# A Fourier transform woven into a gated MLP: the next batch's folds and second-stage calls are put at other steps

## The chip, the cores and the metric

The kernel runs on one core of one Trainium2 chip. The metric is the device time of one execution in microseconds (us), the median over the runs shown. The engines are named as in the profile: PE is TensorE (PEld its weight loads), DVE is VectorE, ACT is ScalarE, POOL is GpSimd, SP is SyncE, which here only issues DMAs. L285 means line 285 of the kernel before.

## The reference, cut to what matters

```python
def _attn_ref(x):                       # x: 8 x 3008 x 256, float32
    X = np.fft.fft(x, axis=1)
    X = np.fft.fft(X, axis=2)
    return X.real.astype(np.float32)

def _moe_ref(x, w_in, w_out):           # x: 24064 x 256, w_in: 256 x 2048, w_out: 2048 x 256
    h = x @ w_in
    g = h * np.cos(h)
    return (g @ w_out).astype(np.float32)
```

The second function is applied to the result of the first, reshaped to 24064 rows of 256.

## The kernel before, in words

**Tiling.** The 8 batches are worked on one after the other. The Fourier transform along the sequence (3008 = 64 x 47) is done in two stages by matmuls with constant matrices; the transform along the 256 columns is folded into `w_in`. Symmetries leave 6 groups of columns per batch (`NG = 6`): group 0 is 225 wide, groups 1 to 5 are 256 wide (`_width`). Each group is passed through the MLP in 8 steps, each with 256 of the 2048 hidden units. So a batch has 48 steps, the kernel 384; below, "index" is the number of a step within its batch, 0 to 47, and group g holds the indices 8g to 8g+7.

**One step.** The main loop (line 741) writes out by hand the order of the instructions of step t; each engine takes its own instructions in that order, and instructions of different engines are tied by waits on the data alone. In step t:

- `mm1(cur, 0)`: two PE matmuls with `WC` into the PSUM tile `H`, which ACT has seeded (L453). `act_e` (L494): ACT copies 2H into `ew`. Then, after four matmuls of another step, `mm1(cur, 1)`: two matmuls with `WS` into the same `H`; they wait until ACT's L494 has read `H`.
- `dve_h` (L499): DVE computes `h = ew - H`. `act_round` (L514): ACT rounds `H` and then `h`, the second half of the work in `h` and both after `dve_h`.
- For the step before: `dve_frac` (L518, twice, one operand `H` in PSUM or `h` in SBUF) and `act_sin` (L524). For the step before that: `dve_g` (L528, twice, again with `H` or `h`) and `dve_s` (L539, L546, L548), differences of SBUF tiles.
- For step t-3: `mm2`, seven PE matmuls into four PSUM banks that accumulate over the 8 steps of a group (L572).

**At the end of a group** (the step whose t-3 or t-4 was a group's last, that is, index 2 and 3 modulo 8): `take_m` (L593) copies the sums from PSUM by ACT, and `combine_m` (L611 to L621) forms the output sums `cb` by six additions on POOL, called at index 3 modulo 8. `store_out`, called at index 4 and at index 5 modulo 8, transposes `cb` on DVE (L664) and issues the output DMAs on SP (L674).

**The next batch's transform.** While batch b is in the MLP, batch b+1 is transformed. `transform(b)` (L360) lists calls with the index of the step at whose end they are put:

- `load_x` (L159): two halves of x, by DMA on SP.
- 8 chunks c, each of 4 of the 32 positions: `fold(b, c, e)` (L240), for e = 0 and 1 one POOL addition or subtraction of 110 x 508 from `xp` into the single buffer `xf`, and with e = 0 an ACT copy of column 0 (L247). `first_half` (L285): PE matmuls from `xf` into the PSUM tile `pz`; ACT copies it to `zs` (L290, L291). For c = 0 and 4 it also runs `middle` (L255, L263). A fold of the next chunk must wait until PE has read `xf`.
- `store_z` (L307): four DMAs on SP per chunk, to DRAM. `load_z` (L316): two DMAs back, as the tile `z2`.
- `second_half(b, g)` (L327): four PE matmuls (eight records) into `pb`, one ACT copy to `pq` (two for g = 0), and two DMAs on SP (L349, L350) that spread one row of it over 128 partitions as `nb`. `pq` and `nb` are what group g of the next batch starts from: `seed` needs `nb` in the step before the group's first.

`pz` and `pb` share one PSUM bank. Batch 0's own transform is done ahead of the loop, but for five `second_half` calls at its indices 5, 10, 14, 18 and 22 (`opening`). Batch 7 has no next batch.

Of the kernel before, what the change touches and what calls it, by code (L numbers as in the profile page):

```python
# [29 lines left out]
NG = 6  # L30
# [91 lines left out]
def kernel(  # L122
# [8 lines left out]
    NB = x.shape[0]  # L131
# [221 lines left out]
    def spread_norm():  # L353
        T = _width(0)
        pq, nb = ready[0, 0]
        pn = psum("pn", "M")
        nc.tensor.matmul(pn[:, 0:T], lhsT=ones, rhs=pq[0:1, T : 2 * T], start=True, stop=True)
        nc.scalar.copy(out=nb[:, 0:T], in_=pn[:, 0:T])

    def transform(b):  # L360
        todo = {}

        def at(o, *call):
            todo.setdefault(o, []).append(call)

        at(3, load_x, b, 0)
        at(14, load_x, b, 1)
        for q in range(4):
            for c, o, f in ((2 * q, 6, 8), (2 * q + 1, 9, 13)):
                at(8 * q + o, fold, b, c, 0)  # L370
                at(8 * q + o, fold, b, c, 1)
                at(8 * q + f, first_half, b, c)
                at(8 * q + f + 1, store_z, b, c, 0)
                at(8 * q + f + 1, store_z, b, c, 1)
        at(39, load_z, b, 0)
        at(39, load_z, b, 1)
        for g in range(NG):
            at(42 + g, second_half, b, g)
        return todo

    def fold_weights(e, n, tag="M"):
        W = WS if e else WC
        pw = psum("pw", tag)
        for i in range(2):
            nc.tensor.matmul(
                pw,
                lhsT=CS[i][:, 128 * e : 128 * e + 128],
                rhs=wr[n][:, 512 * i : 512 * i + 512],  # L390
                start=(i == 0),
                stop=(i == 1),
            )
        cols = slice(512 * n, 512 * n + 512)
        if e:
            nc.scalar.activation(
                out=W[:, cols], in_=pw, func=AF.Copy, bias=0.0, scale=mask[:, 0:1]
            )
            nc.vector.tensor_copy(out=nrow[:, cols], in_=pw[0:1, :])
        else:  # L400
            nc.scalar.copy(out=W[:, cols], in_=pw)
# [76 lines left out]
    def mm1(s, e):  # L478
        T = s.T
        W = WS if e else WC  # L480
        for u in range(2):
            f = 2 * s.fp + u
            nc.tensor.matmul(  # L483
                s.H[:, u * T : u * T + T],
                lhsT=W[:, 128 * f : 128 * f + 128],
                rhs=s.pq[:, e * T : e * T + T],
                start=False,
                stop=True,
                skip_group_check=True,
            )  # L490

    def act_e(s):
        s.ew = spool.tile([128, 512], FP, tag="ew", bufs=2, name="ew")
        nc.scalar.mul(out=s.ew[:, 0 : 2 * s.T], in_=s.H[:, 0 : 2 * s.T], mul=2.0)  # L494
# [21 lines left out]
    def dve_frac(s, sg):  # L516
        r, h = side(s, sg)
        nc.vector.scalar_tensor_tensor(  # L518
            out=r, in0=r, scalar=-BIG, in1=h, op0=ALU.add, op1=ALU.subtract
        )  # L520

    def act_sin(s):
        r = s.r[:, 0 : 4 * s.T]
        nc.scalar.activation(out=r, in_=r, func=AF.Sin, bias=0.0, scale=SIN_SCALE)  # L524

    def dve_g(s, sg):
        r, h = side(s, sg)
        nc.vector.scalar_tensor_tensor(  # L528
            out=r, in0=h, scalar=-0.25, in1=r, op0=ALU.add, op1=ALU.mult
        )  # L530
# [54 lines left out]
    def take_m(s, part):  # L585
        T = s.T
        key = (s.b, s.grp)
        if part == 0:
            mrs[key] = spool.tile([128, 7 * 256], FP, tag="mr", bufs=1, name="mr")
        mv = mrs[key].rearrange("p (m t) -> p m t", m=7)[:, :, 0:T]  # L590
        for k in (2, 3) if part else (0, 1):
            n = 1 if k == 3 else 2
            nc.scalar.mul(  # L593
                out=mv[:, 2 * k : 2 * k + n],
                in_=acc[key][k].rearrange("p (m t) -> p m t", m=2)[:, 0:n, 0:T],
                mul=TWO_PI,
            )

    def combine_m(s):
        T = s.T  # L600
        key = (s.b, s.grp)
        acc.pop(key)
        mv = mrs.pop(key).rearrange("p (m t) -> p m t", m=7)[:, :, 0:T]
        cb = spool.tile([128, 7 * 256], FP, tag="cb", bufs=1, name="cb")
        cf = cb.rearrange("p (m t) -> p m t", m=7)
        cv = [cf[:, m, 256 - T : 256] if m in (2, 3) else cf[:, m, 0:T] for m in range(7)]
        if T < 256:
            nc.gpsimd.memset(cf[:, 0:2, T:256], 0.0)
            nc.gpsimd.memset(cf[:, 2:4, 0 : 256 - T], 0.0)
        tt = nc.gpsimd.tensor_tensor  # L610
        tt(out=cv[0], in0=mv[:, 0], in1=mv[:, 1], op=ALU.add)  # L611
        tt(out=cv[4], in0=mv[:, 0], in1=mv[:, 5], op=ALU.subtract)
        tt(
            out=cf[:, 5:7, 0:T],
            in0=cf[:, 4:5, 0:T].to_broadcast([128, 2, T]),
            in1=mv[:, 3:5],
            op=ALU.add,
        )
        tt(out=cv[1], in0=cv[6], in1=mv[:, 6], op=ALU.add)
        tt(out=cv[2], in0=cv[5], in1=mv[:, 2], op=ALU.add)  # L620
        tt(out=cv[3], in0=cv[5], in1=mv[:, 4], op=ALU.add)  # L621
        outs[key] = cb

    def combine_last(s):
        key = (s.b, s.grp)
        M5, M3 = acc[key][2], acc[key][3]
        mv = mrs.pop(key).rearrange("p (m t) -> p m t", m=7)
        outs[key] = spool.tile([128, 7 * 256], FP, tag="cb", bufs=1, name="cb")
        cv = outs[key].rearrange("p (m t) -> p m t", m=7)
        tt, stt = nc.vector.tensor_tensor, nc.vector.scalar_tensor_tensor  # L630
        more = dict(op0=ALU.mult, op1=ALU.add)
        tt(out=cv[:, 0], in0=mv[:, 0], in1=mv[:, 1], op=ALU.add)
        stt(out=cv[:, 4], in0=M5[:, 256:512], scalar=-TWO_PI, in1=mv[:, 0], **more)
        stt(out=cv[:, 6], in0=M5[:, 0:256], scalar=TWO_PI, in1=cv[:, 4], **more)
        stt(out=cv[:, 1], in0=M3[:, 0:256], scalar=TWO_PI, in1=cv[:, 6], **more)
        store_last(s, 0)
        tt(out=cv[:, 5], in0=cv[:, 4], in1=mv[:, 3], op=ALU.add)
        tt(out=cv[:, 2], in0=cv[:, 5], in1=mv[:, 2], op=ALU.add)
        stt(out=cv[:, 3], in0=M5[:, 0:256], scalar=TWO_PI, in1=cv[:, 5], **more)
        store_last(s, 1)  # L640
# [93 lines left out]
    per = NG * 8  # L734
    n = len(steps)

    def step(t, last=None):
        s = steps[t] if 0 <= t < n else None
        return s if s is not None and (last is None or s.fp == 7) else None

    for t in range(n + LAG + 1):
        cur, prev, old, done = step(t), step(t - 1), step(t - 2), step(t - LAG)
        if cur:
            if t % per == 0:
                todo = transform(cur.b + 1) if cur.b + 1 < NB else {}
            mm1(cur, 0)
            act_e(cur)
            if t == 0:
                spread_norm()
            if t in early:  # L750
                fold_weights(*early[t])
        if t - LAG - 1 == n - 1:
            combine_last(steps[n - 1])
            break
        if step(t - LAG - 1, True):
            take_m(step(t - LAG - 1), 1)
            combine_m(step(t - LAG - 1))
        if done:
            live[0] = (done.b, done.grp)
            mm2(done, 0)  # L760
        if old:
            dve_g(old, 0)
            dve_g(old, 1)
        if step(t + 1):
            seed(step(t + 1))
        if prev:
            dve_frac(prev, 0)
        if old:
            dve_s(old, 0)
        if prev:  # L770
            dve_frac(prev, 1)
            act_sin(prev)
        if old:
            dve_s(old, 1)
        if step(t - LAG, True):
            take_m(done, 0)
        if cur:
            mm1(cur, 1)
        if done:
            mm2(done, 1)  # L780
        if cur:
            dve_h(cur)
            act_round(cur, 0)
            act_round(cur, 1)
        if old:
            dve_s(old, 2)
        if step(t - LAG - 2, True):
            store_out(step(t - LAG - 2), 0)
        if step(t - LAG - 3, True):
            store_out(step(t - LAG - 3), 1)  # L790
        for call in opening.pop(t, ()):
            call[0](*call[1:])
        for call in todo.pop(t % per, ()):
            call[0](*call[1:])


# [28 lines left out]
```

## Time and profile before

| | |
|---|---|
| median of 3 runs | 1974.28 us (1973.58 to 1974.45) |
| profiled execution: its own time | 1975.47 us |
| profiled execution: span | 1973.7 us |
| PE busy | 1946.2 us (99%) |
| DVE busy | 1858.0 us (94%) |
| ACT busy | 1504.2 us (76%) |
| POOL busy | 467.7 us (24%) |
| mean granted PE clock | 0.994 |

The span runs from the first to the last instruction of the core; the profiled execution's own time lies 1.77 us above it. The timeline lists instructions in order of time, with start, duration, engine, line, operation, tiles (out<-in) and shape; neighbours of one kind are merged (x4), and in square brackets stands how long the engine had been idle and what ended that. A matmul in float32 is two records in the trace. The DVE duration of a 128 x 512 operation is some 0.67 us, but the next one starts 0.60 us after it. A busy share is a mean over the whole span.

### The profile page before, as it was taken

To read this page: it belongs to the slowest core of one execution; us is meant where nothing else is said; L and a number is where in the kernel's file an instruction comes from. 1 tells how busy PE (TensorE), PEld (TensorE's weight loads), DVE (VectorE), ACT (ScalarE), POOL (GpSimd) and SP (SyncE) were. 2 spreads that over 40 slices of the span, in tenths; PEclk is the share of its full clock that TensorE was granted. 3 is DMA by queue.
4 is the path that set the end of the run, shared out by engine and by line. 5 is a ranking of instruction groups with operands and counts; after the bars stand their busy time and mean duration, and the time that the engine had idled before them with its cause. 6 is when DMAs were issued, how large, how long until landed. Compare 5 with 4: busy or idle time off the path is not lost.

```text
span 1973.7 us, 28641 instructions
## 1 busy us (share of the span) xinstructions
PE 1946.2 (99%) x9216; PEld 1686.8 (85%) x9216; DVE 1858.0 (94%) x3217; ACT 1504.2 (76%) x2762; POOL 467.7 (24%) x431
## 2 busy tenths in 40 slices
PE   7999999999999999999999999999999999999998
PEld 3888899888988889888898888988889888898887
DVE  4999989999899998999989999999999999899998
ACT  2877777777777778777877777777877787778775
POOL 2133113231133212323122222123311233112111
PEclk7999999999999999999999999999999999999999
DMA  6321121211202012020121101221022200210000
GB/s 196 94 59 29 47 59 27 53 31 51 59 16 59 24 51 58 21 59 23 49 57 28 52 23 53 60 53 25 20 57 59 54 19 21 62 22 10 19 15 22
DMA packets 159957, 88.65 MB, mean 45 GB/s; under 512 B 104845, under 2 KB 150204, under 8 KB 158656
## 3 DMA queue, kind: packets, MB, share of 16 engines
q1 hardware_dynamic: 158320, 85.72, 16.7%
q8 instruction: 74, 1.21, 0.3%
q10 hardware_dynamic: 1392, 1.05, 0.2%
q14 instruction: 75, 0.61, 0.1%
q0 software_dynamic: 96, 0.05, 0.0%
HBM read 49.51 MB, written 37.28 MB: 44 GB/s over the span
## 4 chain that ended last, share of the span: by engine, by line
PE 91%; DVE 5%; DMA 2%; ACT 1%; issue 1%; SPq 0%; ACTq 0%; POOL 0%; DVEq 0%; POOLq 0%
PE M L572 54%; PE H L483 32%; PE pz L285 3%; PE pb L327 2%; DVE r L528 1%; DMA out_dram<-ob 1%; DVE S L548 1%; DVE S L546 1%; DMA xp<-in_x_dram 1%; DVE r L518 0%; DVE S L539 0%; DMA zd<-zs 0%; DVE h L499 0%; DVE ob L664 0%; SPq L674 0%
## 5 line engine op out<-in xcount | busy, mean ns | idle before, releaser
L524 ACT ACTIVATE r<-r 128x1024 f32<-128x1024 f32 (+1 forms) x384 | 398.5, 1038 | 284.3 <-DVE r L518 283.4
L572 PE MATMUL M<-S,VX 128*128 128x256 f32 (+1 forms) x2304 | 612.7, 375 | 0.0
L572 PEld LDWEIGHTS M<-S,VX 128*128 128x128 f32 x2304 | 438.3, 190 | 49.4
L483 PE MATMUL H<-pq,WS 128*128 128x256 f32 (+1 forms) x1536 | 390.8, 377 | 7.8 <-ACT ew L494 7.5
L483 PE MATMUL H<-pq,WC 128*128 128x256 f32 (+1 forms) x1536 | 395.1, 380 | 1.1 <-ACT H L453 1.1
L572 PE MATMUL M<-r,w 128*128 128x256 f32 (+1 forms) x1536 | 387.9, 375 | 0.0
L453 ACT ACTIVATE H<-nb,wn 128x256 f32<-128x256 f32 (+1 forms) x766 | 363.5, 475 | 17.1 <-DVE r L528 3.2
L483 PEld LDWEIGHTS H<-pq,WC 128*128 128x128 f32 x1536 | 284.1, 191 | 73.6 <-ACT r L514 29.2
L499 DVE TENSOR_TENSOR h<-ew,H 128x512 f32<-128x512 f32 (+1 forms) x384 | 257.1, 670 | 87.3 <-PE H L483 81.0
L483 PEld LDWEIGHTS H<-pq,WS 128*128 128x128 f32 x1536 | 290.9, 191 | 49.9 <-ACT ew L494 15.9
L572 PEld LDWEIGHTS M<-r,w 128*128 128x128 f32 x1536 | 300.5, 196 | 27.0
L518 DVE SCALAR_TENSOR_TENSOR r<-r,h 128x512 f32<-128x512 f32 (+1 forms) x384 | 309.7, 806 | 0.0
L240 POOL TENSOR_TENSOR xf<-xp 110x508 f32<-110x508 f32 x112 | 164.9, 1493 | 585.4 <-PE pz L285 540.9
L539 DVE TENSOR_TENSOR S<-r 128x512 f32<-128x512 f32 (+1 forms) x384 | 286.8, 747 | 0.1
L528 DVE SCALAR_TENSOR_TENSOR r<-h,r 128x512 f32<-128x512 f32 (+1 forms) x384 | 272.3, 709 | 0.0
L514 ACT ACTIVATE r<-H 128x512 f32<-128x512 f32 (+1 forms) x384 | 223.0, 581 | 57.1 <-DVE h L499 54.1
L494 ACT ACTIVATE ew<-H 128x512 f32<-128x512 f32 (+1 forms) x384 | 225.7, 588 | 45.5 <-PE H L483 40.3
L518 DVE SCALAR_TENSOR_TENSOR r<-r,H 128x512 f32<-128x512 f32 (+1 forms) x384 | 255.4, 665 | 0.0
L528 DVE SCALAR_TENSOR_TENSOR r<-H,r 128x512 f32<-128x512 f32 (+1 forms) x384 | 254.4, 662 | 0.8 <-ACT r L524 0.8
L514 ACT ACTIVATE r<-h 128x512 f32<-128x512 f32 (+1 forms) x384 | 236.2, 615 | 0.0
L572 PE MATMUL M<-S,w 128*128 128x256 f32 (+1 forms) x768 | 225.4, 375 | 0.0
L572 PE MATMUL M<-r,VX 128*128 128x256 f32 (+1 forms) x768 | 225.2, 375 | 0.0
(79 smaller groups left out, 1497.9 us busy)
## 6 DMA issues: line engine op xcount, KB each, us to landing
out_dram<-ob SPq DMA_DIRECT2D x728, 32.0 KB
xp<-in_x_dram SPq DMA_DIRECT2D x48, 256.0 KB
zd<-zs SPq DMA_DIRECT2D x128, 80.0 KB
z<-zd SPq DMA_DIRECT2D x8, 1280.0 KB
xp<-in_x_dram SPq DMA_DIRECT2D x38, 240.0 KB
nb<-nd SPq DMA_DIRECT2D x40, 128.0 KB
wr<-in_moe_w_in_dram SPq DMA_DIRECT2D x4, 512.0 KB
w<-in_moe_w_out_dram SPq DMA_DIRECT2D x2, 1024.0 KB
```

What stands on the lines that cost most here:

```text
L240: (nc.gpsimd if b else nc.vector).tensor_tensor(out=fv[:, e, :, 1:128], in0=xv[:, :, 1:128], in1=xv[:, :, 255:128:-1], op=ALU.subtract if ...
L285: nc.tensor.matmul(pz[rows, a:512], lhsT=w, rhs=fv[:, e, a:512], start=True, stop=True)
L453: nc.scalar.activation(out=s.H[:, u * T : u * T + T], in_=s.nb[:, 0:T], func=AF.Copy, bias=0.25, scale=wn[:, f : f + 1],)
L483: nc.tensor.matmul(s.H[:, u * T : u * T + T], lhsT=W[:, 128 * f : 128 * f + 128], rhs=s.pq[:, e * T : e * T + T], start=False, stop=True, ...
L494: nc.scalar.mul(out=s.ew[:, 0 : 2 * s.T], in_=s.H[:, 0 : 2 * s.T], mul=2.0)
L499: nc.vector.tensor_tensor(out=s.h[:, 0 : 2 * T].rearrange("p (u t) -> p u t", u=2)[:, :, ::-1], in0=s.ew[:, 0 : 2 * T].rearrange("p (u t) ...
L514: nc.scalar.activation(out=r, in_=h, func=AF.Copy, bias=BIG, scale=1.0)
L518: nc.vector.scalar_tensor_tensor(out=r, in0=r, scalar=-BIG, in1=h, op0=ALU.add, op1=ALU.subtract)
L524: nc.scalar.activation(out=r, in_=r, func=AF.Sin, bias=0.0, scale=SIN_SCALE)
L528: nc.vector.scalar_tensor_tensor(out=r, in0=h, scalar=-0.25, in1=r, op0=ALU.add, op1=ALU.mult)
L539: nc.vector.tensor_tensor(out=sv[:, 0:2], in0=gv[:, 2:3].to_broadcast([128, 2, T]), in1=gv[:, 0:4:3], op=ALU.subtract,)
L572: nc.tensor.matmul(acc[key][m // 2][:, 256 * (m % 2) : 256 * (m % 2) + T], lhsT=w, rhs=a, start=first, stop=s.fp == 7, skip_group_check=True,)
```

## The change

The main loop no longer looks calls up by the index within the batch but by the step's absolute number, so that a call may be put into the batch that follows. The table holds, for q = 0 to 3, the index at whose end each call is put; chunks 2q ("even") and 2q+1 ("odd") are listed apart.

| call | before | after |
|---|---|---|
| fold, even chunk, e = 0 and e = 1 | 8q+6 and 8q+6 | 8q+7 and 8q+8 |
| fold, odd chunk, e = 0 and e = 1 | 8q+9 and 8q+9 | 8q+13 and 8q+14 |
| first_half, even and odd chunk | 8q+8 and 8q+13 | 8q+9 and 8q+15 |
| store_z, even and odd chunk | 8q+9 and 8q+14 | 8q+10 and 8q+16 |
| load_z | 39 | 41 |
| second_half, g = 0 to 5 | 42, 43, 44, 45, 46, 47 | 43, 49, 52, 59, 69, 77 |

Indices from 48 on lie in the batch that follows: 49 is its index 1, 52 is 4, 59 is 11, 69 is 21, 77 is 29. No instruction is added or taken away.

```diff
+    todo = {}
+
     def transform(b):
-        todo = {}
+        t0 = (b - 1) * NG * 8
 
         def at(o, *call):
-            todo.setdefault(o, []).append(call)
+            todo.setdefault(t0 + o, []).append(call)
 
         at(3, load_x, b, 0)
         at(14, load_x, b, 1)
         for q in range(4):
-            for c, o, f in ((2 * q, 6, 8), (2 * q + 1, 9, 13)):
-                at(8 * q + o, fold, b, c, 0)
-                at(8 * q + o, fold, b, c, 1)
-                at(8 * q + f, first_half, b, c)
-                at(8 * q + f + 1, store_z, b, c, 0)
-                at(8 * q + f + 1, store_z, b, c, 1)
-        at(39, load_z, b, 0)
-        at(39, load_z, b, 1)
-        for g in range(NG):
-            at(42 + g, second_half, b, g)
-        return todo
+            for c, o in ((2 * q, 8 * q + 7), (2 * q + 1, 8 * q + 13)):
+                at(o, fold, b, c, 0)
+                at(o + 1, fold, b, c, 1)
+                at(o + 2, first_half, b, c)
+                at(o + 3, store_z, b, c, 0)
+                at(o + 3, store_z, b, c, 1)
+        at(41, load_z, b, 0)
+        at(41, load_z, b, 1)
+        for g, o in enumerate((43, 49, 52, 59, 69, 77)):
+            at(o, second_half, b, g)
...
-            if t % per == 0:
-                todo = transform(cur.b + 1) if cur.b + 1 < NB else {}
+            if t % per == 0 and cur.b + 1 < NB:
+                transform(cur.b + 1)
...
-        for call in todo.pop(t % per, ()):
+        for call in todo.pop(t, ()):
             call[0](*call[1:])
```

## The prediction

> **What bounds the kernel now.** First the page's busy times, then the stretches of the timeline. Batches 1 to 6 have equal windows; batch 7 has no next batch to transform. Columns: window, its length, busy us (instructions) of PE, PEld, DVE, ACT, POOL, PE clock, DMA share, GB/s.
>
> ```profile
> PE 1946.2 (99%) x9216; PEld 1686.8 (85%) x9216; DVE 1858.0 (94%) x3217; ACT 1504.2 (76%) x2762; POOL 467.7 (24%) x431
> 721.60:962.40 240.80, 239.59 (x1147) 208.93 (x1146) 230.38 (x397) 187.55 (x347) 60.74 (x54) 1.00 0.17 43
> 1684.80:1925.60 240.80, 240.80 (x1160) 217.93 (x1159) 229.69 (x417) 188.11 (x336) 37.37 (x38) 1.00 0.10 25
> ```
>
> PE is the bound, at full clock; a transformed batch loses only about 1.2 us of 240.8 visibly. Where that is, the starts of the L483 matmuls with WC tell (the difference of two starts is a step). In batch 7 a full 256-wide step is 4.75 us, always. In batch 3 a second_half adds 0.89 (5.64), a first_half 1.10 and 0.10 in the step after (5.85, 4.85). The only steps without such work that are longer than in batch 7 lie in group 0: indices 5, 6, 7 take 5.11, 4.96, 4.51 against 4.18, 4.26, 4.41, so 0.93 + 0.70 + 0.10 = **1.73 us**. The same steps repeat in batches 1 to 6; in batch 0 they are missing, since its first fold waits for x until 72.0. Index 4 and 5 of batch 3 show why:
>
> ```profile
> 789.55 1.11 POOL L621 TENSOR_TENSOR cb<-cb,mr 128x256 f32<-128x256 f32 x1
> 790.62 3.02 POOL L240 TENSOR_TENSOR xf<-xp 110x508 f32<-110x508 f32 x2
> 791.07 1.46 DVE L546 TENSOR_TENSOR S<-S,r 128x225 f32<-128x225 f32 x1
> 792.45 0.61 DVE L499 TENSOR_TENSOR h<-ew,H 128x450 f32<-128x450 f32 x1
> 792.98 0.92 DVE L548 TENSOR_TENSOR S<-r,S 128x225 f32<-128x225 f32 x1
> 794.00 0.54 ACT L494 ACTIVATE ew<-H 128x450 f32<-128x450 f32 x1
> 794.59 0.65 PE L483 MATMUL H<-pq,WS 128*128 128x225 f32 x2 [0.65 <-ACT ew L494]
> ```
>
> The two folds start right behind the last output sum. While POOL runs them, DVE's operations with both inputs in SBUF stretch: L546 from 0.38 (batch 7) to 1.46, L548 from 0.38 to 0.92, together 1.62; L499, with one input in PSUM, stays at 0.61. Then `h` is late, so ACT's `ew` is late, so PE's WS matmuls wait. The important thing is *when* the folds ran: they are put at the end of step 6, and ran in step 4. POOL isn't held to a step; it takes its next instruction when its data allow. What kept the other folds off the output sums is a wait for PE:
>
> ```profile
> 868.14 1.23 POOL L621 TENSOR_TENSOR cb<-cb,mr 128x256 f32<-128x256 f32 x1
> 876.57 1.26 POOL L240 TENSOR_TENSOR xf<-xp 110x508 f32<-110x508 f32 x1 [7.20 <-PE pz L285]
> POOL xf L240 <- PE pz L285: 540.9, 49, 18.1
> ```
>
> **The change, part by part.** *Folds of odd chunks.* Put at 8q+13, they now stand in POOL's queue behind combine_m of 8q+11. PE has by then read `xf` (first_half of the even chunk, 8q+9), so no wait for PE is left. POOL finishes combine_m in step 8q+12 and starts both folds there at once; that e = 1 is put a step later holds nothing. So the pattern of group 0 returns in groups 1 to 4. *Even chunks* from c = 2 still wait for PE (first_half at 8q+7), run at index 0 of groups 2 to 4 with 1.10 us of first_half just ahead, and cost nothing, like the folds at index 1 before. *Chunk 0* has no PE wait: as before, it runs behind the sums in group 0, whatever its place says.
>
> Price in a 256-wide group, from batch 7, where combine_m runs without folds (index 19 to 23):
>
> ```profile
> 1825.72 1.23 POOL L621 TENSOR_TENSOR cb<-cb,mr 128x256 f32<-128x256 f32 x1
> 1827.42 0.41 DVE L546 TENSOR_TENSOR S<-S,r 128x256 f32<-128x256 f32 x1
> 1827.76 0.68 DVE L499 TENSOR_TENSOR h<-ew,H 128x512 f32<-128x512 f32 x1
> 1828.36 0.41 DVE L548 TENSOR_TENSOR S<-r,S 128x256 f32<-128x256 f32 x1
> 1839.23 0.58 ACT L494 ACTIVATE ew<-H 128x512 f32<-128x512 f32 x1
> 1840.26 1.03 PE L483 MATMUL H<-pq,WS 128*128 128x256 f32 x4
> ```
>
> L621 ends at 1826.95. Folds of 1.49 and 1.37 behind it, as in group 0: L546 starts at 1828.44 instead of 1827.42 (+1.02), L548 at 1829.81 instead of 1829.38 (+0.43). DVE is pushed back **1.45 us**. The slack between the end of L494 and PE's WS matmuls in the three steps that follow is 0.69, 0.56, 0.45 (the last: 1839.81 to 1840.26), less some 0.05 for the hand-over (794.54 to 794.59 above). L494 comes late by 1.02, 1.45, 1.45, and in the second also by L247's column copy (0.19), which now stands ahead of it. PE so loses, in total by each step, 0.38, 1.13, 1.05: **1.13 us** a group with nothing else in it.
>
> *second_half as a cover.* Its 0.89 is work that PE must do anyway; put where DVE is behind, it fills the gap. Batches 1 to 6: group 1 (index 11): DVE, 0.82 behind there, gets back to 0.10, so 1.13 - 0.72 = 0.4. Groups 2 and 3 (index 21, 29): 0.89 ahead of the second due time, but ACT's `pq` copy (0.59) also comes ahead of L494: 1.13 + 0.59 - 0.89 = 0.83 each. Group 4: none, 1.13. Group 0 (index 4): DVE sets the pace there, so the 0.89 is free, and L247's move from step 6 to 7 gives back 0.08: -0.97. Sum 0.4 + 0.83 + 0.83 + 1.13 - 0.97 = 2.2 a batch, x6 = 13.3. Batch 0: `opening`'s second_half at index 10 covers some 0.35 of group 1, the later ones come too late: 0.8 + 3 x 1.13 = 4.1. Batch 7 gets five second_halves and batch 6 gives up as many: 0. **Sum +17.4 us.**
>
> *The rest costs nothing*, with this cover. SP: the DMAs of second_half at index 1 now stand ahead of load_x; they wait for `pq`, so load_x is issued from about 781.7 instead of 771.86 (batch 3's clock). It lands 8.4 later (DMA engines busy 772 to 780.2), at about 790; chunk 0's fold wants it at 791.5. If it came later, that fold would leave the sums, a gain of up to 1.73 a batch. `nb`: the shortest notice is 43 to seed at 47, 19 us, against about 5 for copy and two DMAs. `z2`: the last store at 40, load at 41, use at the end of 43, some 13 us; its 1.5 MB take 6 at the 272 GB/s of load_x. The output DMAs wait about 2 us behind second_half at 4, 21 and 29; transposes have two `ob` buffers and a group to spare. `pz` and `pb` never meet in a step.
>
> The unknown is the 1.45. Fold pairs behind first_half cost DVE 1.00 (876.57) and 1.73 (851.62). With 1.00 in place of 1.45, every loss shrinks by 0.45 (to no less than 0): 0 + 0.38 + 0.38 + 0.68 - 0.97 = 0.5, x6 + 2.4 = +5. With 1.73, 28 pairs x 0.28 more: +25. I keep 1.45, since group 0's own 1.62, in the same place in POOL's queue, is nearest.
>
> **The sum.** Against the profiled execution's own time, 1975.47 + 17.4 = 1992.9. The median of the runs lies 1.19 lower: 1974.28 + 17.4 = **1991.7**.
>
> **Rivals.**
> 1. *Not slower: the slack absorbs the folds* (12%). If the port is less in the way than in group 0, only the cover of group 0 stays: -0.97 x 6 = -5.8, 1968.5. The point is where 28 losses equal that gain: at a push of about 0.75 us a pair. For it: DVE was up to 0.95 late in batch 3 with no loss. Against: no fold pair whose DVE rows I followed cost less than 1.00.
> 2. *The change does what its places say* (5%): folds of chunk 0 leave group 0, odd folds run one in step 14, one in step 15, where DVE recovers 0.47 a step. -1.73 x 6 = -10.4, and some 0.3 lost in groups 1 and 4, and 0.3 in each of batch 0: +4.8; 1968.7. Against: the fold that ran two steps before its place.
> 3. *POOL keeps the port* (8%): DVE's L518, waiting at L621's end (1826.29, 1.21 long), is passed over by the first fold too. Another 1.0 us or so a pair, 28 pairs: +28, so 2020. Against: in batch 3 L518, from 790.00, was through at 791.15, ahead of the first fold's end. The Trainium skill ("SBUF — State Buffer", Who interferes with whom) says that a DVE instruction with two SBUF inputs and a GpSimd instruction that reads SBUF lock each other out, and that the one issued first holds the port throughout. By that rule nothing but issue order would choose between my sum and this rival; the stretched L546 beside the unstretched L499 agrees with it.
> 4. *In between* (8%): a push of 0.65 to 0.85, within 0.2%.
>
> The forecast has 67%. Within 0.2% (3.9 us) is about what a measurement of this kernel can't tell from no change. Faster 0.16, same 0.09, slower 0.75. The range leaves out rivals 1, 2 and part of 3: from 1975 (push 0.8) to 2004 (push 1.73, +25, and half of the 1.3 a batch that second_half covers in groups 1 to 3 missing, +4).
>
> **What the profile after would show.** POOL's L240 directly behind L621 in groups 0 to 4 (right), or after a wait or a gap (wrong). POOL's waits for PE before L240 fall to about three a batch. PE's waits for ACT L494 rise from 13 to some 50. L546 near 1.4 at index 12, 20, 28, 36; steps 13 to 15, 21 to 23, 29 to 31, 37 to 39 too long by about 0.4, 0.8, 0.8, 1.1 in all; group 0's index 4 to 7 longer only by what is left of 0.89. Wrong if load_x lands after the sums in group 0, or if the 256-wide steps stay at 4.75.

## The result, and the profile after

The changed kernel takes 2024.65 us against 1974.43 us (medians of six runs each): 50.2 us more, a ratio of 1.0253 (95% interval 1.024 to 1.0267). The prediction (1991.7) had the sign, one of the two causes, and a third of the size.

Behind `transform` the changed kernel's lines are lower by one: L498 is what was L499 (`h`), L493 was L494 (`ew`), L610 to L620 were L611 to L621 (the output sums), L592 was L593 (ACT's copies of the sums), L517 was L518, L538 was L539, L545 was L546, L547 was L548, L571 was L572. The page of the changed kernel, with its windows of batch 3 and of batch 7 to the end (columns as before: window, length, busy us of PE, PEld, DVE, ACT, POOL, PE clock, DMA share, GB/s):

```profile
PE 1959.6 (97%) x9216; PEld 1679.7 (83%) x9216; DVE 1898.5 (94%) x3217; ACT 1498.8 (74%) x2762; POOL 481.3 (24%) x431
786.00:1034.20 248.20, 241.67 (x1148) 208.05 (x1147) 236.72 (x397) 186.49 (x346) 62.74 (x54) 1.00 0.16 42
1776.80:2022.50 245.70, 238.69 (x1147) 215.50 (x1145) 230.21 (x416) 182.61 (x323) 37.41 (x38) 1.00 0.08 18
```

The instructions are the same ones, at the same clock; a transformed batch is 248.2 long instead of 240.8, and DVE is busy 6.3 us longer in it with the same 397 instructions. The waits of POOL and of PE (engine, line, what ended the wait; us in total, times, longest):

```profile
POOL xf L240 <- PE pz L285: 348.6, 21, 17.3
...
PE H L482 <- ACT ew L493: 42.2, 60, 1.4
```

PE's wait for `ew` in the kernel before:

```profile
PE H L483 <- ACT ew L494: 7.5, 13, 0.7
```

As predicted, only three folds a batch still wait for PE (21; 49 before), and PE's WS matmuls wait for ACT's `ew` 60 times (13 before). The steps say where. The table gives for each group of batch 3 its length less PE's own work, against the prediction. PE's own work is the length of the same group in the run no_folds_delay below, which has the same work for PE and in which no step of these groups is lengthened by a late engine:

| group | PE's own | lost, by the prediction | lost, changed kernel | lost, run after_delay (below) |
|---|---|---|---|---|
| 0 | 36.34 | 1.04 | 1.87 | 1.01 |
| 1 | 40.36 | 0.4 | 0.90 | 0.92 |
| 2 | 41.29 | 0.83 | 2.13 | 0.82 |
| 3 | 41.40 | 0.83 | 2.14 | 0.82 |
| 4 | 40.40 | 1.13 | 2.38 | 1.24 |

Before, only group 0 of batch 3 lost anything: 2.01 (36.57, less 36.34 without its two second_halves of 0.89). Of this 1.71 are by the folds (36.57 against 34.86 in batch 7; the prediction's 1.73) and 0.30 by the sums alone; the table's 1.04 is 2.01 less the predicted 0.97. Group 2 of the changed kernel, batch 3, index 18 to 21, in the timeline:

```profile
879.94 0.69 DVE L498 TENSOR_TENSOR h<-ew,H 128x512 f32<-128x512 f32 x1 [1.57 <-ACT r L523]
880.42 0.73 POOL L610 TENSOR_TENSOR cb<-mr 128x256 f32<-128x256 f32 x1 [11.48 <-ACT mr L592]
880.54 0.89 DVE L547 TENSOR_TENSOR S<-r,S 128x256 f32<-128x256 f32 x1
883.19 1.23 POOL L611 TENSOR_TENSOR cb<-mr 128x256 f32<-128x256 f32 x1 [2.04 <-ACT mr L592]
883.76 1.21 DVE L517 SCALAR_TENSOR_TENSOR r<-r,h 128x512 f32<-128x512 f32 x1
884.50 1.60 POOL L612 TENSOR_TENSOR cb<-cb,mr 128x512 f32<-128x512 f32 x1
884.89 1.49 DVE L545 TENSOR_TENSOR S<-S,r 128x256 f32<-128x256 f32 x1
887.87 1.24 POOL L620 TENSOR_TENSOR cb<-cb,mr 128x256 f32<-128x256 f32 x1
889.06 3.45 POOL L240 TENSOR_TENSOR xf<-xp 110x508 f32<-110x508 f32 x2
889.64 1.75 DVE L517 SCALAR_TENSOR_TENSOR r<-r,h 128x512 f32<-128x512 f32 x1
891.31 1.48 DVE L545 TENSOR_TENSOR S<-S,r 128x256 f32<-128x256 f32 x1
895.07 1.13 PE L482 MATMUL H<-pq,WS 128*128 128x256 f32 x4 [1.39 <-ACT ew L493]
```

The last five lines are the prediction: the folds directly behind the last sum, DVE's two-SBUF-input operations stretched (0.68 to 1.75, 0.41 to 1.48), PE waiting for `ew`. The six lines ahead of them are not in it: **the sums themselves** already stretch L547 (0.89), L517 (1.21) and L545 (1.49). The same operations in batch 7 of the kernel before, index 18 and 19:

```profile
1817.66 0.69 DVE L499 TENSOR_TENSOR h<-ew,H 128x512 f32<-128x512 f32 x1 [0.39 <-PE H L483]
1818.26 0.42 DVE L548 TENSOR_TENSOR S<-r,S 128x256 f32<-128x256 f32 x1
1818.58 0.73 POOL L611 TENSOR_TENSOR cb<-mr 128x256 f32<-128x256 f32 x1 [30.25 <-ACT mr L593]
1820.99 0.69 DVE L518 SCALAR_TENSOR_TENSOR r<-r,h 128x512 f32<-128x512 f32 x1
1821.05 1.22 POOL L612 TENSOR_TENSOR cb<-mr 128x256 f32<-128x256 f32 x1 [1.73 <-ACT mr L593]
1821.60 0.95 DVE L546 TENSOR_TENSOR S<-S,r 128x256 f32<-128x256 f32 x1
```

There the three take 0.42, 0.69 and 0.95, together 2.06; after the change 3.59, so 1.53 more. Call *lateness* the time from the end of PE's WS matmuls to the start of `h` on DVE in the same step; some 0.1 is none. At index 19 it is 1.73, where batch 7 of the kernel before has 0.17, so 1.56 more; at index 20 it is 2.91.

What differs ahead of the sums: their first, L610, starts 4.31 after the start of the step's WC matmuls instead of 4.65, since ACT's L592 starts 3.66 after it instead of 4.0. The step before (index 17) carries a first_half now, 1.10 us of PE work in which DVE and ACT catch up: ahead of `h` of index 18 DVE has been idle for 1.57 instead of 0.39. L547, which used to start 0.32 ahead of the first sum (1818.26 against 1818.58), now starts 0.12 behind it.

**Theory A**, two causes: the folds behind the sums, as predicted, and PE work at index 1 of a group (first_half at 8q+9, second_half at 49), which makes the sums start some 0.35 us early and meet DVE's operations one by one. **Theory B**, one cause: the folds' place behind the sums costs 2.1 to 2.4 us by itself, and what stands at index 1 is harmless.

### The profile page after: what moved, and what is told of

It is laid out like the page before. It is cut to its first block, busy times and chain, and to the rows that moved or that the text cites. A ratio compares the mean times of both kernels' runs of the same rounds, so it can differ in the third digit from the quotient of the medians.

```text
span 2022.5 us, 28674 instructions
## 1 busy us (share of the span) xinstructions
PE 1959.6 (97%) x9216; PEld 1679.7 (83%) x9216; DVE 1898.5 (94%) x3217; ACT 1498.8 (74%) x2762; POOL 481.3 (24%) x431
## 3 DMA queue, kind: packets, MB, share of 16 engines
q8 instruction: 74, 1.21, 0.3%
## 4 chain that ended last, share of the span: by engine, by line
PE 73%; DVE 17%; issue 4%; ACT 4%; DMA 1%; ACTq 0%; POOL 0%; DVEq 0%; POOLq 0%; SPq 0%
PE M L571 42%; PE H L482 26%; DVE r L527 4%; DVE S L545 4%; PE pz L285 3%; DVE h L498 3%; DVE S L538 2%; DVE r L517 2%; ACT r L513 2%; DVE S L547 2%; PE pb L327 2%; ACT ew L493 1%; DMA xp<-in_x_dram 1%; DMA zd<-zs 0%; ACT r L523 0%
## 5 line engine op out<-in xcount | busy, mean ns | idle before, releaser
L571 PE MATMUL M<-S,VX 128*128 128x256 f32 (+1 forms) x2304 | 612.6, 375 | 0.0
L571 PEld LDWEIGHTS M<-S,VX 128*128 128x128 f32 x2304 | 438.4, 190 | 49.4
L482 PE MATMUL H<-pq,WS 128*128 128x256 f32 (+1 forms) x1536 | 396.6, 381 | 42.2 <-ACT ew L493 42.2
L571 PE MATMUL M<-r,w 128*128 128x256 f32 (+1 forms) x1536 | 387.9, 375 | 0.0
L482 PEld LDWEIGHTS H<-pq,WS 128*128 128x128 f32 x1536 | 284.5, 190 | 105.5 <-ACT ew L493 73.6
L498 DVE TENSOR_TENSOR h<-ew,H 128x512 f32<-128x512 f32 (+1 forms) x384 | 257.0, 669 | 96.3 <-PE H L482 54.9
L517 DVE SCALAR_TENSOR_TENSOR r<-r,h 128x512 f32<-128x512 f32 (+1 forms) x384 | 331.2, 862 | 0.0
L571 PEld LDWEIGHTS M<-r,w 128*128 128x128 f32 x1536 | 300.5, 196 | 27.0
L538 DVE TENSOR_TENSOR S<-r 128x512 f32<-128x512 f32 (+1 forms) x384 | 274.3, 714 | 0.1
L240 POOL TENSOR_TENSOR xf<-xp 110x508 f32<-110x508 f32 x112 | 178.5, 1614 | 395.2 <-PE pz L285 348.6
L610 POOL TENSOR_TENSOR cb<-mr 128x256 f32<-128x256 f32 (+1 forms) x47 | 35.4, 753 | 957.9 <-ACT mr L592 957.9
L527 DVE SCALAR_TENSOR_TENSOR r<-h,r 128x512 f32<-128x512 f32 (+1 forms) x384 | 263.2, 685 | 0.0
L517 DVE SCALAR_TENSOR_TENSOR r<-r,H 128x512 f32<-128x512 f32 (+1 forms) x384 | 255.5, 665 | 0.0
L493 ACT ACTIVATE ew<-H 128x512 f32<-128x512 f32 (+1 forms) x384 | 225.3, 587 | 38.8 <-PE H L482 34.0
L545 DVE TENSOR_TENSOR S<-S,r 128x256 f32<-128x256 f32 (+1 forms) x384 | 226.8, 591 | 0.0
```

The source lines that it names most:

```text
L240: (nc.gpsimd if b else nc.vector).tensor_tensor(out=fv[:, e, :, 1:128], in0=xv[:, :, 1:128], in1=xv[:, :, 255:128:-1], op=ALU.subtract if ...
L482: nc.tensor.matmul(s.H[:, u * T : u * T + T], lhsT=W[:, 128 * f : 128 * f + 128], rhs=s.pq[:, e * T : e * T + T], start=False, stop=True, ...
L498: nc.vector.tensor_tensor(out=s.h[:, 0 : 2 * T].rearrange("p (u t) -> p u t", u=2)[:, :, ::-1], in0=s.ew[:, 0 : 2 * T].rearrange("p (u t) ...
L517: nc.vector.scalar_tensor_tensor(out=r, in0=r, scalar=-BIG, in1=h, op0=ALU.add, op1=ALU.subtract)
L527: nc.vector.scalar_tensor_tensor(out=r, in0=h, scalar=-0.25, in1=r, op0=ALU.add, op1=ALU.mult)
L538: nc.vector.tensor_tensor(out=sv[:, 0:2], in0=gv[:, 2:3].to_broadcast([128, 2, T]), in1=gv[:, 0:4:3], op=ALU.subtract,)
```

## The experiments

All times are medians; the kernel before, measured beside each run, took 1974.1 to 1974.3. In brackets stands the ratio to it with its 95% interval.

**1. odd_behind: the odd chunks alone.** Edit to the changed kernel:

```diff
-            for c, o in ((2 * q, 8 * q + 7), (2 * q + 1, 8 * q + 13)):
+            for c, f0, f1, h in ((2 * q, 7, 7, 8), (2 * q + 1, 13, 13, 15)):
...
+                at(8 * q + f0, fold, b, c, 0)
+                at(8 * q + f1, fold, b, c, 1)
+                at(8 * q + h, first_half, b, c)
-        for g, o in enumerate((43, 49, 52, 59, 69, 77)):
+        for g, o in enumerate((43, 44, 45, 46, 47, 48)):
```

> Only the odd chunks are moved as in the change (folds at 8q+13, first_half at 8q+15); even chunks keep first_half at 8q+8, their folds are put at 8q+7; second_half at 43 to 48, one a step. So the odd folds stand behind the output sums on POOL, but no first_half stands at index 1 of a group. Theory A (two causes: the odd folds behind the sums, and first_half at index 1, one step ahead of the sums, which lets DVE run ahead so that the sums themselves meet DVE's two-SBUF-input operations): each of groups 1 to 4 loses 1.1 us as the prediction worked out, 28 x 1.1 = 32, so about 2006, and L499 starts no more than 0.3 after PE's WS matmuls at index 3 of a group. Theory B (the place behind the sums alone makes the whole loss): 2.2 to 2.4 us a group as measured after the change, 28 x 2.3 = 64, so about 2038.

Measured: 2013.49 us (1.0207, 1.0192 to 1.0223). At index 19 the lateness is 0.17, as A has it, at index 20 1.78 (the prediction's 0.71 + 1.02 = 1.73), and groups 2 to 4 lose 1.25 each (predicted 1.13). Group 1 loses 2.0 instead of 1.1, which makes up most of what A's 2006 lacks. Its rows, index 12 of batch 3:

```profile
844.55 2.93 POOL L240 TENSOR_TENSOR xf<-xp 110x508 f32<-110x508 f32 x2
844.59 1.77 DVE L538 TENSOR_TENSOR S<-r 128x512 f32<-128x512 f32 x1
846.28 1.75 DVE L517 SCALAR_TENSOR_TENSOR r<-r,h 128x512 f32<-128x512 f32 x1
```

The sums of the 225-wide group end earlier in the step, so each fold meets a 512-wide two-input operation just starting, and holds it up for most of its own length: 1.09 + 1.07 instead of 1.45 in all. So the price of the same pair of folds runs from 1.0 to 2.2, by where DVE stands.

**2. first_at_9: the even first_half alone**, with second_half as in 1:

```diff
-            for c, f0, f1, h in ((2 * q, 7, 7, 8), (2 * q + 1, 13, 13, 15)):
+            for c, f0, f1, h in ((2 * q, 6, 6, 9), (2 * q + 1, 10, 10, 13)):
```

> Only the even chunks' first_half is moved as in the change (8q+9); the odd folds stand at 8q+10, ahead of the output sums on POOL, odd first_half at 8q+13 as before; second_half at 43 to 48. Theory A: the sums slip against DVE (L499 some 1.7 late at index 3, as after the change), but the slack and first_half at index 5 take up most of it: 0 to 0.4 us a group, 1974 to 1985. Theory B: no slip of the sums (L499 at most 0.3 late at index 3), 1974.

Measured: 1974.81 us (1.0009, 0.9999 to 1.0019), no difference. The time fits both theories. A's 1.7 late at index 3 is missed: it is 0.58 to 0.68 in groups 1 to 4. B's bound of 0.3 is missed too. Here the odd folds run at index 2 (852.38 to 855.31), slow DVE down there, and so ACT's copies start late (4.6 after WC), not early. So first_half at index 1 cost nothing where the folds follow it at index 2; runs 3 and 7 below show its harm where *nothing follows it* there.

**3. both_plain: the change without the spread** of second_half.

```diff
-        for g, o in enumerate((43, 49, 52, 59, 69, 77)):
+        for g, o in enumerate((43, 44, 45, 46, 47, 48)):
```

> The change with second_half left at one a step (43 to 48), so that nothing covers the loss in groups 1 to 4 and group 0 is as before. Theory A and B: 2.4 us in each of groups 1 to 4 (the measured loss of group 4, where the change has no second_half), 28 x 2.4 = 67, so about 2041. If it comes out near the changed kernel's 2024.6 or below, second_half put at 49 to 77 covers nothing or costs something.

Measured: 2033.42 us (1.031, 1.0295 to 1.0325). Groups 2 to 4 lose the 2.4 expected, group 1 only 1.8 in place of 2.4, and batch 0 loses 6.5 in place of 9.6. Against odd_behind, whose odd folds stand in the same place, 1.13 us in each of groups 2 to 4 come with the even first_half at index 1 and not 0. Spreading second_half saves 8.8 us of this.

**4. spread_only: second_half alone**, on the folds and first_half of before (shown against the kernel before; the lookup by the step's absolute number is that of the change):

```diff
-        at(39, load_z, b, 0)
-        at(39, load_z, b, 1)
-        for g in range(NG):
-            at(42 + g, second_half, b, g)
+        at(41, load_z, b, 0)
+        at(41, load_z, b, 1)
+        for g, o in enumerate((43, 49, 52, 59, 69, 77)):
+            at(o, second_half, b, g)
```

> Only second_half is moved as in the change (43, 49, 52, 59, 69, 77; load_z at 41); folds, first_half and store_z as before. As the prediction priced it, the call at index 4 of group 0 covers 0.89 us of its 1.73 in six batches: 1974.3 - 5.3 = 1969. Theory A: the call at index 1 makes the sums of group 0 slip as first_half at index 1 does, and eats the cover: 1973 to 1975, with L499 over 1.0 late at index 3 of group 0, against 0.15 before.

Measured: 1987.03 us (1.0072, 1.0057 to 1.0087); neither number. A defect of the experiment: at index 21 and 29 second_half and an odd first_half fall into one step, and `pb` and `pz` share one PSUM bank:

```profile
878.42 0.57 ACT L343 COPY pq<-pb 128x512 f32<-128x512 f32 x1
879.14 1.08 PE L285 MATMUL pz<-xf,LCS 110*64 110x512 f32 x4 [1.13 <-ACT pq L343]
```

Those steps take 7.9 instead of 5.85 + 0.89, 1.2 too much, 14.4 in twelve of them. In group 0 A held: 1.52 late at index 3, and nearly the whole cover of index 4 eaten in batches 1, 3, 4 and 5 (38.28 against 36.57 + 2 x 0.89). In batches 2 and 6 chunk 0's folds start 0.49 and 1.13 behind the last sum, and less is lost.

**5. spread_clean: the same without the collision and with 48 for 49.** Edit to run 4:

```diff
-        for g, o in enumerate((43, 49, 52, 59, 69, 77)):
+        for g, o in enumerate((43, 48, 52, 59, 70, 78)):
```

> The kernel before with second_half at 43, 48, 52, 59, 70, 78: as in the run that only spread it, but never in the same step as a first_half (index 22 and 30 instead of 21 and 29), and at index 0 instead of 1. If the two steps of 7.9 us there were pz waiting for ACT to clear the one bank that pb held: they fall back to 5.85 and 4.75 + 0.89, 2 x 1.2 x 6 = 14.4 less than 1987. Theory A: with no call at index 1 the sums of group 0 do not slip, and index 4 covers its 0.89: 1969. If index 0 is as bad as index 1: 1973 to 1974.

Measured: 1969.58 us (0.9979, 0.9969 to 0.999). The 7.9 us steps are gone, and 0.14 is the lateness at index 3 of group 0. The cover at index 4 is worth the prediction's 0.89 a batch, if nothing stands at index 1.

**6. behind_spread: the change as the prediction reckoned it**, by an edit to run 1:

```diff
-        for g, o in enumerate((43, 44, 45, 46, 47, 48)):
+        for g, o in enumerate((43, 48, 52, 59, 69, 77)):
```

> The odd chunks as in the change (folds behind the sums, first_half at 8q+15), even first_half at 8q+8, second_half spread as in the change but at index 0 instead of 1 of the next batch (48 instead of 49). By theory A this is the change as the prediction reckoned it, without the slip of the sums: 1991.7 by its sum; with group 1 as the run of odd folds alone measured it (1.98 instead of the 1.1 ahead of the cover), some 1996. By theory B it is near the changed kernel, 2018 to 2025.

Measured: 1996.44 us (1.0112, 1.0097 to 1.0127). Groups 2 and 3 lose 0.83 and 0.82 (predicted 0.83), group 0 gains 0.98 (predicted 0.97), and batch 0 loses 4.15 (predicted 4.1); group 1 loses 1.06 in place of 0.4. Without PE work at index 1 the prediction's sum is 22.3 in place of 17.4; with it, 50.2.

**7. no_folds: the changed kernel without its folds** (those of batches 1 to 7 are left out, so its output is not the reference's):

```diff
-    nc.gpsimd.memset(xf[0:XR, 512:1024:128], 0.0)
+    nc.gpsimd.memset(xf[0:XR], 0.0)
...
-        (nc.gpsimd if b else nc.vector).tensor_tensor(
+        if b == 0:
+            nc.vector.tensor_tensor(
```

> The changed kernel without the POOL folds of batches 1 to 7 (left out; xf holds zeros there, and the output of those batches is not the reference's). A kernel with no loss beyond PE's own work would take 1974.3 - 10.4 = 1964. Theory A: the sums still meet DVE's operations one step after first_half at index 1, L499 is 1.7 late at index 3 of groups 2 to 4 and some 2 late in the step after, at a loss of 0 to 0.5 us a group: 1964 to 1976. Theory B: with no folds nothing is late, L499 at most 0.3 late at index 3, 1964.

Measured: 1975.16 us (1.0006, 0.9996 to 1.0016). With no fold at all, `h` is 1.72 late at index 3 of groups 2 to 4, and the next step takes 5.22 instead of 4.75. B falls: with no folds it has nothing left that could be late. The next run shows what the kernel takes without this lateness: 1961.8.

**8. no_folds_delay and after_delay: the sums put back.** To the run without folds, and to the changed kernel itself, one ACT copy is added that nothing needs:

```diff
         if step(t - LAG, True):
+            if t % per < 40 and 0 < t < (NB - 1) * per:
+                nc.scalar.copy(out=dly, in_=LCS[:, 0:384])
             take_m(done, 0)
```

> The run without folds, and one ACT copy of 128 x 384 (some 0.35 us, into a tile that nothing reads) put ahead of take_m's first part in groups 0 to 4 of batches 0 to 6: it gives back the 0.35 us by which ACT's copies of the sums, and with them POOL's first addition, start earlier after a first_half at index 1. If that earlier start is what makes the sums meet DVE's two-SBUF-input operations: L499 is back at about 0.2 late at index 3 of groups 2 to 4 and step 4 at 4.75, 28 x 0.4 less than 1975.2, so 1964 to 1967. If DVE's own running ahead makes it, whatever POOL's start: 1975.

> The changed kernel with the same ACT copy ahead of take_m's first part. Nothing is taken off any engine; ACT gets some 0.35 us more per group. If the earlier start of the sums is what the prediction had missed: the sums run as in the prediction, and the loss falls to that of the run with even first_half at index 0 and second_half at 48, 1996, or a few us more; if not, 2024.6 or more.

Measured: 1961.83 us without folds (13.3 less), and **1995.13 us** for the changed kernel (1.0102, 1.0086 to 1.0118): work added to ACT takes away 29.5 of the 50.2 us. The copy takes 0.50 and puts the first sum back by 0.42 (4.73 after the WC matmuls, against 4.31), a little more than the 0.35 meant. Index 18 and 19 of its batch 3 (its lines are those of before):

```profile
867.52 0.42 DVE L548 TENSOR_TENSOR S<-r,S 128x256 f32<-128x256 f32 x1
867.82 0.73 POOL L611 TENSOR_TENSOR cb<-mr 128x256 f32<-128x256 f32 x1 [11.89 <-ACT mr L593]
870.26 0.69 DVE L518 SCALAR_TENSOR_TENSOR r<-r,h 128x512 f32<-128x512 f32 x1
870.28 1.25 POOL L612 TENSOR_TENSOR cb<-mr 128x256 f32<-128x256 f32 x1 [1.73 <-ACT mr L593]
870.86 0.95 DVE L546 TENSOR_TENSOR S<-S,r 128x256 f32<-128x256 f32 x1
```

L548 is again ahead of the first sum and takes 0.42 in place of 0.89. DVE, about half a microsecond earlier from there on, has started L518 20 ns ahead of the second sum: 0.69 in place of 1.21. The lateness at index 19 is 0.18 in place of 1.73. Ahead of `h` of index 18 DVE sits just as idle as in the changed kernel (1.56 and 1.57 us), so it isn't DVE's running ahead but POOL's start against it.

**9. after48: the changed kernel with 48 for 49.**

```diff
-        for g, o in enumerate((43, 49, 52, 59, 69, 77)):
+        for g, o in enumerate((43, 48, 52, 59, 69, 77)):
```

> The changed kernel with one number altered: second_half of group 1 at 48 instead of 49, so at index 0 of the next batch. Theory A: the sums of group 0 no longer slip and the call at index 4 covers its 0.89 in six batches: about 5 less than the changed kernel, 2019.6. Theory B (the call at index 1 is harmless): 2024.6.

Measured: 2020.6 us (1.0231, 1.0213 to 1.0249), 4.1 less. Group 0 falls from 38.21 to 37.37, a loss of 1.02; the gain comes in the batches 1 to 4 above all, since in batch 6 of the changed kernel group 0 had lost only 0.50 as it was. There chunk 0's folds start 1.04 us behind the last sum:

```profile
1552.82 2.79 POOL L240 TENSOR_TENSOR xf<-xp 110x508 f32<-110x508 f32 x2 [1.04 <-PE M L571]
```

In batches 2, 3 and 5 they wait 0.38, 0.24 and 0.48 for the load of x, which stands behind second_half's DMAs on SP; that this is also what held batch 6 is likely, but the row names another.

**10. early_fold0: a version faster than both.** The kernel before; from batch 2 on, chunk 0 is folded in group 5 of the batch ahead, where each step has 0.89 us of second_half (the loop calls `transform` 28 steps earlier for it):

```diff
-        at(3, load_x, b, 0)
+        early0 = b > 1
+        at(-24 if early0 else 3, load_x, b, 0)
...
+                f = -2 if early0 and c == 0 else 8 * q + f0
```

> The kernel before with one thing moved: from batch 2 on, chunk 0's fold stands at index 46 of the batch ahead (and its half of x is loaded at index 24 there), so that it no longer runs behind the output sums in group 0; it runs in group 5, where each step carries 0.89 us of second_half. If the 1.73 us at index 5 to 7 of group 0 is the fold behind the sums: 6 x 1.73 = 10.4 less, 1964, and index 5 to 7 at 4.18, 4.26, 4.41. If the sums alone make it: 1974.

Measured: 1964.15 us (0.9949, 0.9934 to 0.9963), 10.0 less than before. The folds still run directly behind the sums, now those of group 4 (lines higher by one than before):

```profile
981.25 1.24 POOL L622 TENSOR_TENSOR cb<-cb,mr 128x256 f32<-128x256 f32 x1
982.44 3.12 POOL L240 TENSOR_TENSOR xf<-xp 110x508 f32<-110x508 f32 x2
```

The lateness there is 0.36 at most, group 5 takes 43.34 as before, and index 5 to 7 of group 0 take 4.19, 4.27 and 4.41. The place behind the sums is harmless here, where PE has other work in the same steps.

## Why the prediction was right and wrong, point by point

- *Odd folds land directly behind the output sums, whatever their place in the program says*: right. The folds placed at 8q+13 and 8q+14 start behind the last sum with no gap in groups 1 to 4.
- *DVE is pushed back 1.45, PE loses 1.13 a group*: nearly right where the sums run as before: PE loses 1.25 (runs 1 and 6). In the changed kernel the pair cost DVE 2.14 (1.07 on L517 and 1.07 on L545), since both were blocked in full. With the sums put back the loss is 1.24 again (group 4 in run 8), so this too follows from the sums' lateness.
- **The step that failed** is "Price in a 256-wide group, from batch 7, where combine_m runs without folds". The price left the sums where they stand in batch 7, and the sum has no term for moving the even first_half from 8q+8 to 8q+9, nor for a second_half at 49: both counted as PE time alone. They stand one step ahead of the sums, with nothing at index 2 behind them. The runs showed 1.56 us more lateness at index 3 from the sums alone (run 7 has it without a fold), 1.13 us a group of it for PE (run 3 against run 1), and 29.5 of the 50.2 us go when the sums are put back by 0.42 us.
- *The second_half at index 4 covers 0.97 in group 0*: it covered 0.14 in batch 3. The cause is the same, the call at 49; at 48 the cover is there (runs 5, 6, 9).
- *Groups 2 and 3: 0.83*: right without the slip (0.82 to 0.83), 2.1 with it.
- *Group 1: 0.4*: too small even without the slip, 0.9 to 1.1; its sums are shorter, so the folds meet other operations. This is most of what run 6 has above the prediction's sum (22.3 against 17.4).
- *Batch 0: 4.1*: it is 2.1 longer and has five second_halves of 0.89 fewer, so it lost 6.5; without the slip 4.15 (run 6).
- *The rest costs nothing*: no cost of it shows, but one sign of being wrong came true. The load of x was issued 12.4 us after the batch's start (12.2 reckoned), yet in batches 2, 3 and 5 chunk 0's folds waited for it behind the sums, and by batch 6 they ran 1.04 behind them; group 0 lost 1.33 and 0.50 in batches 5 and 6, against 1.87 in batch 3. It is a gain, as the prediction said of that case.
- The prediction's second window, 1684.80 to 1925.60, is not batch 7 alone: batch 7 starts at 1732.65, so the window holds the end of batch 6 with its second_halves. The step lengths on which the price rests are read from batch 7 itself.
- Rival 3, POOL keeping the port, came near in size (2020), but by luck: it has no term for the sums' slip. In the changed kernel L517 is indeed blocked through the first fold, but because it starts 0.58 behind it; in run 1, where it had started ahead, it got through first. The rule quoted from the Trainium skill ("SBUF — State Buffer", Who interferes with whom), that the instruction issued first keeps the port throughout, agrees with the rows: 20 ns ahead of the second sum L518 took 0.69, and 0.57 behind it L517 took 1.21.

## What to carry to other kernels

A place in the program holds an engine to nothing: to say where an instruction runs, name the wait that holds it, and read what stands ahead of it in its own queue. When two engines hold each other up, as DVE and POOL do here, a move is priced by which operations then meet, and work that ends a step early is a change as much as work that is late; look for what starts when an engine has caught up. Where the bound engine has work that must be done anyway, put it in the very steps in which the others fall behind, and not a step ahead of them.

## What the runs showed that was not expected

- A start some 0.35 us earlier on POOL cost 1.56 us on DVE by the next step. L547 started 0.12 us too late to be ahead of it, and each operation behind it then started 0.4 to 0.6 us behind the next POOL instruction (L517 behind L611, L545 behind L612).
- Adding one ACT copy of 0.50 us to each of groups 0 to 4 made the changed kernel 29.5 us faster.
- Two matmul groups that share a PSUM bank and fall into one step cost 1.2 us (run 4): PE waits until ACT has copied the first, and ACT began that copy only 0.41 us after the first group's end.
